# Gated linear attention followed by a tanh-shrink MLP: handing the tree products of a unit to the scheduler about a unit ahead

## The chip, the cores and the metric

One core of a Trainium2 chip. The metric is device time in microseconds (us), lower is better; every time below is of one run of the whole kernel or of its profiled execution. The engines are named as in the profile: PE (TensorE, matmuls and transposes), DVE (VectorE), ACT (ScalarE), POOL (GpSimd) and SP, whose queue issues all the DMAs of this kernel. TensorE's clock is granted at one of two levels, 1.2 or 2.4 GHz; the profile gives it as a share of 2.4 GHz.

## The reference

```python
# attention: B, H, S, D = 4, 8, 768, 48
for t in range(S):
    state = alpha[:, :, t, :, None] * state + np.einsum('bhd,bhe->bhde', k[:, :, t], v[:, :, t])
    y[:, :, t] = np.einsum('bhd,bhde->bhe', q[:, :, t], state)
# bridge
x = y.transpose(0, 2, 1, 3).reshape(B * S, H * D)          # 3072 x 384
# MLP: w_in 384 x 2048, w_out 2048 x 384, both float64 in memory
h = x @ w_in
g = h - np.tanh(h)
out = (g @ w_out).astype(np.float32)
```

## The kernel before, in words

The work is cut into 12 **units** of 256 tokens, three to a batch entry, numbered 0 to 11; a unit is two **chunks** of 128 tokens. For each unit there is a recurrence (`gla`) and an MLP (`moe`). The MLP of unit u needs the recurrence of unit u, and the recurrence of a unit needs the state left by the unit before it in the same batch entry.

The recurrence of a unit is a Python generator that yields after each step, 18 steps in all:

- **Tree** (lines 237 to 252, 8 steps). PE transposes `alpha` of both chunks (`tp<-ident,an`), ACT copies the result to `pre`, and POOL works through seven levels, at each multiplying halves of `suf` (L250) and of `pre` (L251): the cumulative products of alpha from the left and from the right. 14 POOL instructions of 128x512 in a chain, a copy among them, and a memset (L247, L248).
- **Ends** (lines 253 to 261, 1 step). DVE clamps the last products into `ends` (L254) and inverts them into `recs` (L257); POOL scales `suf` by `recs` (L259, two instructions).
- **Chunks** (lines 264 to 317, 4 steps each). PE transposes q and k of the chunk, DVE multiplies them with `pre` and `suf` into `qh` and `kh` (L267, L268), PE forms the scores `sc` (L274), DVE masks them into `x` (L278), PE transposes `kh` (L284), forms `y` from the old state (L291) and from `x` (L296) and the update `up` (L305), and the state is updated: DVE adds (L313), POOL multiplies by the chunk's end (L314, two halves). The first chunk of a batch entry has no old state (L316 on DVE alone), the last one needs no update.
- The last step also sends the transposed result to `xT` with DMAs (L324).

The MLP of a unit (`dense`) has 8 steps and a closing one. A step `s` computes `h` with PE (L119), then the activation on ACT and DVE; DVE's part per step is `w` (L127), `d` (L129), `z` (L132), `g` (L133) and `g` again (L134). Two steps later, `second(s)` multiplies `g` with `w_out` (L141) into `o`. There are two PSUM buffers for `h`, so `h` of a step can be written when `d` of the step two before it has been read.

Ahead of the MLP the float64 weights are decoded to float32 in 28 pieces (`load_w`): five DVE instructions (L181 to L188), two on ACT, one on POOL (`man`, L191), and a last one on DVE (L192).

Two things set the order. The code at line 335 gives each step a place in a list: the unit of place is one MLP step, an MLP with its closing step takes `MOE` = 9 places, unit u's MLP begins at place 9u, and all steps are emitted in the order of their places. Then a scheduler places what was emitted on each engine's queue, and may move an instruction ahead of earlier emitted ones where it reckons that it is ready; each engine then works through its queue strictly in that order. Before the change the 18 steps of a recurrence stand half a place apart:

```python
at = (u - 1) * MOE - EARLY
order += [(at + i * MOE / GLA, 0, "gla", u) for i in range(GLA)]
order += [(at - 4, 0, "load", u)]
```

Of the kernel before, what the change touches and what calls it, by code (L numbers as in the profile page):

```python
# [18 lines left out]
CU = 2  # L19
# [17 lines left out]
def kernel(  # L37
# [18 lines left out]
    LEVELS = 7  # L56
# [3 lines left out]
    FS = FT // 2  # L60
# [96 lines left out]
    def main(ctx):  # L157
# [174 lines left out]

        MOE, GLA, EARLY = FS + 1, 3 + LEVELS + 4 * CU, 5.0
        order = []
        for u in range(NU):
            order += [(u * MOE + i, 1, "moe", u) for i in range(MOE)]
            at = (u - 1) * MOE - EARLY
            order += [(at + i * MOE / GLA, 0, "gla", u) for i in range(GLA)]  # L340
            order += [(at - 4, 0, "load", u)]
        order += [(-MOE - EARLY + 2 + i, 2, "weights", 0) for i in range(2 * d_ff // 512)]
        make = {"moe": moe, "gla": gla, "load": load, "weights": lambda _: weights()}
# [130 lines left out]
    with ExitStack() as inner:  # L474
        main(inner)
# [52 lines left out]
```

## Time and profile before

| | before |
|---|---|
| time, median of 3 runs (lowest to highest) | 851.12 us (850.72 to 852.2) |
| time of the profiled execution | 853.7 us |
| its span, first to last instruction | 852.0 us |
| PE busy | 690.9 us (81%) |
| DVE busy | 555.4 us (65%) |
| ACT busy | 362.4 us (43%) |
| POOL busy | 295.4 us (35%) |
| mean granted TensorE clock | 0.914 |

The span is what the profile covers, and 1.7 us of the execution's time lie around it. Busy shares are averages over two stages that differ: to about 165 us the weights are decoded and PE is often idle; after that PE is busy nearly all the time but for a pause in each unit.

### The profile page before, as it was taken

What the parts mean: (1) busy time and instruction counts of PE and PEld (TensorE: products, weight loads), DVE (VectorE), ACT (ScalarE), POOL (GpSimd) and SP (SyncE); (2) the same over time, 40 slices, a digit from 0 to 9 for tenths busy, and PEclk for the clock granted to TensorE, in tenths of its full rate; (3) what the DMA queues carried; (4) which work ended last, traced back from release to release, by engine and by line L of the source; (5) the groups of instructions that cost most, each with busy time, mean ns of one, the idle gap of its engine ahead of it and who ended that gap; (6) DMA issues with size and microseconds to landing.
All of it is one profiled execution on the core that took longest, in us unless ns stands there. A gap on an engine that the chain in (4) does not pass through costs nothing.

```text
span 852.0 us, 10194 instructions
## 1 busy us (share of the span) xinstructions
PE 690.9 (81%) x3698; PEld 494.3 (58%) x3698; DVE 555.4 (65%) x818; ACT 362.4 (43%) x629; POOL 295.4 (35%) x281
## 2 busy tenths in 40 slices
PE   1172642697999979979989899799799799799995
PEld 1151431474767747747657567567577477577673
DVE  4979989966666557557467457556656656565573
ACT  2131331462645525615425435526444445355552
POOL 6739468272000630720710801802703604500000
PEclk9985765898999989989989989989899899899998
DMA  9571744500102202212112112013021000000000
GB/s 158 118 177 56 177 127 105 121 0 17 31 0 56 47 15 54 45 34 49 30 38 45 31 37 62 13 41 72 0 47 29 0 20 19 0 20 19 19 1 22
DMA packets 113911, 41.62 MB, mean 49 GB/s; under 512 B 102592, under 2 KB 110272, under 8 KB 113856
## 3 DMA queue, kind: packets, MB, share of 16 engines
q1 hardware_dynamic: 113856, 40.91, 21.2%
q8 instruction: 31, 0.51, 0.2%
q14 instruction: 24, 0.20, 0.1%
HBM read 31.46 MB, written 4.72 MB: 42 GB/s over the span
## 4 chain that ended last, share of the span: by engine, by line
PE 55%; POOL 20%; DVE 16%; ACT 3%; issue 3%; DMA 1%; SPq 1%; DVEq 0%; POOLq 0%; ACTq 0%
PE o L141 21%; PE h L119 20%; POOL pre L251 9%; POOL suf L250 9%; PE tp L234 4%; PE sc L274 3%; PE y L296 3%; PE y L291 2%; DVE g L134 2%; DVE e L186 2%; DVE e L184 2%; DVE g L133 2%; DVE e L181 1%; DVE w_in L192 1%; DVE m L188 1%
## 5 line engine op out<-in xcount | busy, mean ns | idle before, releaser
L141 PE MATMUL o<-w_out,g 128*128 128x384 f32 x768 | 284.2, 520 | 43.6 <-DVE g L134 42.9
L119 PE MATMUL h<-xT,w_in 128*128 128x256 f32 x1152 | 283.5, 390 | 22.8 <-DMA xT<-yT 14.2
L119 PEld LDWEIGHTS h<-xT,w_in 128*128 128x128 f32 x1152 | 215.5, 194 | 66.0 <-issue 13.6
L141 PEld LDWEIGHTS o<-w_out,g 128*128 128x128 f32 x768 | 154.5, 204 | 145.1 <-DVE g L134 49.5
L125 ACT ACTIVATE sq<-h 128x512 f32<-128x512 f32 x96 | 57.3, 597 | 192.7 <-PE h L119 153.4
L314 POOL TENSOR_TENSOR state<-state,pre 64x192 f32<-64x192 f32 x32 | 19.9, 622 | 314.4 <-DVE state L313 312.4
L127 DVE TENSOR_TENSOR w<-h,sq 128x512 f32<-128x512 f32 x96 | 65.8, 685 | 84.8 <-ACT th L126 84.8
L251 POOL TENSOR_TENSOR pre<-pre 128x512 f32<-128x512 f32 x84 | 97.9, 1166 | 5.3
L250 POOL TENSOR_TENSOR suf<-suf,pre 128x512 f32<-128x512 f32 x72 | 94.9, 1318 | 5.5
L134 DVE COPY_PREDICATED g<-large,d 128x512 f32<-128x512 int32 x96 | 86.7, 903 | 2.6
L132 DVE SCALAR_TENSOR_TENSOR z<-sq,z 128x512 f32<-128x512 f32 x96 | 71.1, 740 | 23.7 <-ACT z L130 23.7
L133 DVE SCALAR_TENSOR_TENSOR g<-z,w 128x512 f32<-128x512 f32 x96 | 81.7, 851 | 3.1
L131 ACT ACTIVATE large<-sq,m_bias 128x512 f32<-128x512 f32 x96 | 69.1, 720 | 5.6 <-DVE g L134 5.6
L128 ACT ACTIVATE z<-sq,z_bias 128x512 f32<-128x512 f32 x96 | 69.4, 723 | 2.9 <-DVE g L133 2.9
L130 ACT ACTIVATE z<-z,g_bias 128x512 f32<-128x512 f32 x96 | 68.7, 716 | 0.0
L234 PE MATMUL tp<-ident,kn 128*128 128x128 f32 x96 | 17.8, 315 | 59.9 <-DVE qh L267 59.9
L129 DVE TENSOR_TENSOR d<-h,th 128x512 f32<-128x512 f32 x96 | 65.2, 679 | 0.0
L126 ACT ACTIVATE th<-h 128x512 f32<-128x512 f32 x96 | 56.9, 593 | 0.0
L234 PEld LDWEIGHTS tp<-ident,kn 128*128 128x128 f32 x96 | 11.9, 156 | 67.7 <-DVE qh L267 61.2
L191 POOL TENSOR_TENSOR man<-man,low 128x384 f32<-128x384 f32 (+1 forms) x28 | 33.6, 1200 | 48.1 <-ACT man L189 48.1
L254 DVE TENSOR_SCALAR ends<-pre 128x8 f32<-128x8 f32 x12 | 2.0, 168 | 73.3 <-POOL pre L251 73.3
L189 ACT ACTIVATE man<-m 128x384 f32<-128x384 int32 (+1 forms) x28 | 15.9, 570 | 79.5 <-DVE m L188 79.5
(59 smaller groups left out, 603.0 us busy)
## 6 DMA issues: line engine op xcount, KB each, us to landing
raw<-in_moe_w_in_dram SPq DMA_DIRECT2D x12, 512.0 KB, 4.2
raw<-in_moe_w_out_dram SPq DMA_DIRECT2D x16, 384.0 KB, 3.2
an<-in_alpha_dram SPq DMA_DIRECT2D x24, 192.0 KB, 4.1
kn<-in_k_dram SPq DMA_DIRECT2D x24, 192.0 KB, 3.2
qn<-in_q_dram SPq DMA_DIRECT2D x24, 192.0 KB, 3.3
vn<-in_v_dram SPq DMA_DIRECT2D x24, 192.0 KB, 3.6
out_dram<-ob SPq DMA_DIRECT2D x24, 192.0 KB, 1.9
xT<-yT SPq DMA_DIRECT2D x72, 48.0 KB, 2.0
```

The costliest lines, as they stand in the source:

```text
L119: T.matmul(h[:, a, :], lhsT=w_in[:, j, f * P:(f + 1) * P], rhs=x_t[:, j, :], start=(j == 0), stop=(j == KT - 1))
L127: V.tensor_mul(w, h, sq)
L128: A.activation(z, sq, AF.Square, bias=z_bias, scale=ZA)
L129: V.tensor_sub(d, h, th)
L130: A.activation(z, z, AF.Square, bias=g_bias)
L131: A.activation(large, sq, AF.Relu, bias=m_bias)
L132: V.scalar_tensor_tensor(out=z, in0=sq, scalar=ZL, in1=z, op0=ALU.mult, op1=ALU.add)
L133: V.scalar_tensor_tensor(out=g, in0=z, scalar=ZC, in1=w, op0=ALU.add, op1=ALU.mult)
L134: V.copy_predicated(out=g, mask=large.bitcast(I32), data=d)
L141: T.matmul(o[c], lhsT=g[:, a * tu + c * P:a * tu + (c + 1) * P], rhs=w_out[:, f, :], start=(f == 0), stop=(f == FT - 1))
L250: GP.tensor_mul(s0, s0, e1)
L251: GP.tensor_mul(p1, p1, e0)
```

## The change

The 18 steps of a recurrence are split into two runs. The first 8 (the tree) are emitted from place 9(u-1) - 8 on, 0.4 places apart; the other 10 (ends, both chunks, the DMAs of xT) from place 9(u-1) on, also 0.4 apart. Before, all 18 were emitted from place 9(u-1) - 5 on, 0.5 apart. So the tree of unit u is now emitted among the chunk steps of unit u-1, whose places are 9(u-2) to 9(u-2) + 3.6. The loads of a unit stand 4 places ahead of its tree, as before, and so 3 places earlier than they did; the weights start 3 places earlier too. No instruction is added, removed or altered, and no buffer is added.

```diff
-        MOE, GLA, EARLY = FS + 1, 3 + LEVELS + 4 * CU, 5.0
+        MOE, TREE, CHUNK, EARLY = FS + 1, 1 + LEVELS, 2 + 4 * CU, 8.0
         order = []
         for u in range(NU):
             order += [(u * MOE + i, 1, "moe", u) for i in range(MOE)]
             at = (u - 1) * MOE - EARLY
-            order += [(at + i * MOE / GLA, 0, "gla", u) for i in range(GLA)]
+            order += [(at + 0.4 * i, 0, "gla", u) for i in range(TREE)]
+            order += [((u - 1) * MOE + 0.4 * i, 0, "gla", u) for i in range(CHUNK)]
             order += [(at - 4, 0, "load", u)]
```

What the scheduler makes of it is seen in the queues of the two built programs, at unit 8 as an example.

DVE's queue before, around the `ends` of unit 8, which stands between `d` and `z` of an MLP step:

```order
L127 TENSOR_TENSOR w<-h,sq 128x512
L129 TENSOR_TENSOR d<-h,th 128x512
L254 TENSOR_SCALAR ends<-pre 128x8
L257 RECIPROCAL recs<-ends 128x8
L132 SCALAR_TENSOR_TENSOR z<-sq,z 128x512
L133 SCALAR_TENSOR_TENSOR g<-z,w 128x512
L134 COPY_PREDICATED g<-large,d 128x512
```

DVE's queue now at the same instruction (`x_3358` and `x_3359` are the masked scores of the second chunk of unit 7):

```order
L132 SCALAR_TENSOR_TENSOR z<-sq,z 128x512
L278 TENSOR_TENSOR x_3358<-sc_3348,keep 128x512
L278 TENSOR_TENSOR x_3359<-sc_3349,keep 128x512
L133 SCALAR_TENSOR_TENSOR g<-z,w 128x512
L254 TENSOR_SCALAR ends<-pre 128x8
L134 COPY_PREDICATED g<-large,d 128x512
L257 RECIPROCAL recs<-ends 128x8
L127 TENSOR_TENSOR w<-h,sq 128x512
L129 TENSOR_TENSOR d<-h,th 128x512
```

The `ends` of unit 8 was emitted at place 63, after the chunks of unit 7; the scheduler has moved it forward, into the second chunk of unit 7, ahead of the last instruction of an MLP step.

POOL's queue before, from the state products of unit 7 (`state_91` of its first chunk, `state_90` of its second) to the start of the tree of unit 8:

```order
L259 TENSOR_TENSOR suf<-suf,recs 128x512 x2
L314 TENSOR_TENSOR state_91<-state_91,pre 64x4x48 x2
L314 TENSOR_TENSOR state_90<-state_90,pre 64x4x48 x2
L247 COPY suf<-pre 128x512
L248 MEMSET suf 128x512
L251 TENSOR_TENSOR pre<-pre 128x512
L250 TENSOR_TENSOR suf<-suf,pre 128x256x2
```

POOL's queue now, from the start of the tree of unit 8:

```order
L247 COPY suf<-pre 128x512
L251 TENSOR_TENSOR pre<-pre 128x512
L250 TENSOR_TENSOR suf<-suf,pre 128x256x2
L314 TENSOR_TENSOR state_91<-state_91,pre 64x4x48
L251 TENSOR_TENSOR pre<-pre 128x256x2
L314 TENSOR_TENSOR state_91<-state_91,pre 64x4x48
L250 TENSOR_TENSOR suf<-suf,pre 128x128x4
```

The tree of unit 8 now begins ahead of the state products of unit 7's first chunk, which stand inside it; those of the second chunk stand behind the whole tree and the scaling of `suf`.

PE's queue before at the transposes of `an` (alpha) of unit 8, between MLP steps:

```order
L234 MATMUL tp<-ident,an_72 128x128 x4
L119 MATMUL h<-xT,w_in 128x256 x2
L234 MATMUL tp<-ident,an_72 128x128 x4
L119 MATMUL h<-xT,w_in 128x256 x4
```

PE's queue now at the same transposes (`x_3249` and `x_3250` are the masked scores of the first chunk of unit 7):

```order
L284 MATMUL tp<-ident,kh 128x128 x4
L291 MATMUL y<-qh,state_90 64x128 x8
L296 MATMUL y<-x_3249,vn_79 64x128
L234 MATMUL tp<-ident,an_72 128x128 x4
L296 MATMUL y<-x_3250,vn_79 64x128
...
L234 MATMUL tp<-ident,an_72 128x128 x4
L296 MATMUL y<-x_3250,vn_79 64x128
```

They have moved to where unit 7's first chunk forms its `y`. From the second of them to the `second` step that needs the `g` behind `ends`, PE's queue now holds three MLP `h` steps (L119), two `second` steps (L141), and of unit 7's recurrence two `up` (L305), the transposes of q and k, the scores, the transposes of `kh` and both parts of `y` of the second chunk.

In the first part of the program, the tree of unit 3 now stands among the last weights on POOL and DVE; before, only units 0 to 2 stood there and unit 3's came after the last weight. Unit 4 takes the place there that unit 3 had.

## Rows read from the trace of the kernel before

**Rows 1.** Waits of the whole span: us in total, times, longest us.

```profile
DVE ends L254 <- POOL pre L251: 73.3, 9, 9.2
PE o L141 <- DVE g L134: 42.9, 8, 5.5
```

**Rows 2.** Timeline of DVE from 395 to 432 us: start, us, idle before and releaser.

```profile
425.58 0.17 DVE L254 TENSOR_SCALAR ends<-pre 128x8 f32<-128x8 f32 x1 [8.01 <-POOL pre L251]
...
428.02 1.45 DVE L134 COPY_PREDICATED g<-large,d 128x512 f32<-128x512 int32 x1
...
431.99 0.73 DVE L134 COPY_PREDICATED g<-large,d 128x512 f32<-128x512 int32 x1
```

**Rows 3.** Timeline of POOL from 395 to 432 us: one unit's tree.

```profile
407.60 0.65 POOL L247 COPY suf<-pre 128x512 f32<-128x512 f32 x1 [16.27 <-ACT pre L239]
...
412.51 1.60 POOL L250 TENSOR_TENSOR suf<-suf,pre 128x512 f32<-128x512 f32 x1
...
424.49 1.06 POOL L251 TENSOR_TENSOR pre<-pre 128x512 f32<-128x512 f32 x1
```

**Rows 4.** Timeline of PE from 366 to 432 us, around the same tree.

```profile
406.19 0.66 PE L234 MATMUL tp<-ident,an 128*128 128x128 f32 x4
...
421.33 2.75 PE L119 MATMUL h<-xT,w_in 128*128 128x256 f32 x12
429.52 2.92 PE L141 MATMUL o<-w_out,g 128*128 128x384 f32 x4 [5.44 <-DVE g L134]
```

**Rows 5.** Chain that ended last: start, us, what; `x8` and `x12` are one MLP step.

```profile
307.01 10.72 PE o L141 x24
...
369.01 10.44 PE o L141 x24
...
776.06 2.58 PE o L141 x8
778.64 2.59 PE h L119 x12
```

**Rows 6.** Stretches of 1 us: engines' busy time, granted clock, DMA share, GB/s.

```profile
428.00:429.00 1.00, 0.00 (x0) 0.00 (x0) 0.98 (x1) 0.72 (x1) 0.88 (x1) 0.78 0.00 0
...
729.00:730.00 1.00, 0.67 (x3) 0.05 (x1) 0.00 (x0) 1.00 (x2) 0.92 (x2) 1.00 0.00 0
732.00:733.00 1.00, 0.00 (x0) 0.00 (x0) 0.00 (x0) 0.00 (x0) 0.92 (x2) 0.68 0.00 0
```

**Rows 7.** Chain that ended last, 380 to 400 us: pieces of a chunk.

```profile
383.34 0.59 PE tp L284 x4
...
388.62 0.60 PE up L305 x16
...
390.28 0.44 PE tp L234 x4
...
391.58 0.57 PE tp L234 x4
...
393.88 1.09 PE sc L274 x16
...
397.75 1.02 PE y L291 x16
398.78 0.87 PE y L296 x16
```

**Rows 8.** Groups of instructions of the whole span, by line: busy, mean ns.

```profile
L314 POOL TENSOR_TENSOR state<-state,pre 64x192 f32<-64x192 f32 x32 | 19.9, 622 | 314.4 <-DVE state L313 312.4 <-PE tp L234 1.3
L267 DVE TENSOR_TENSOR qh<-tp,pre 128x512 f32<-128x512 f32 x24 | 16.5, 688 | 36.8 <-PE tp L234 36.1
L259 POOL TENSOR_TENSOR suf<-suf,recs 128x512 f32<-128x512 f32 x24 | 33.4, 1408 | 7.6 <-DVE recs L257 7.6
```

**Rows 9.** Stretches of 20 us while weights are decoded: PE, PEld, DVE, ACT, POOL busy.

```profile
40.00:60.00 20.00, 14.56 (x107) 11.02 (x108) 17.34 (x39) 7.70 (x14) 5.89 (x6) 0.91 0.78 178
60.00:80.00 20.00, 7.55 (x42) 4.95 (x41) 17.81 (x17) 3.51 (x7) 19.30 (x18) 0.59 0.27 78
```

## The prediction

> **What bounds the kernel now.** I read the page first, then the chain that ended last, then the waits, then the timelines of DVE, POOL and PE side by side over one unit. The kernel has two stages. Once the weights are decoded, PE is the bound: the chain runs through its matmuls, one MLP step of `h` in 2.59 us and one of `o` in 2.58 [rows 5], with one hole per unit. Ahead of that DVE is the bound: in the 20 us from 60 it is busy for 17.81 and PE for 7.55 [rows 9].
>
> The hole is made by one instruction. DVE waits 73.3 us in all, in nine waits, at `ends` (L254) for POOL's tree [rows 1]. In the unit shown POOL starts the tree at 407.60 and ends it at 425.55, 18.0 us; DVE has nothing before it but 8.01 us of waiting, though the MLP's own `z`, `g`, `g` stand right behind it. They end at 429.47, 3.9 us after `ends` began [rows 2, 3]. PE ran without a gap to 424.08 and then waits 5.44 us for that `g` [rows 4]. The clock goes too: it falls to 1.2 GHz within the pause, so that the 24 `o` matmuls behind it take 10.44 to 10.72 us, where 3 x 2.58 = 7.74 is the full-clock price [rows 5]. One hole therefore costs 5.44 + 2.85 = 8.3 us; nine of them (units 3 to 11), 74.7 us.
>
> **The change, part by part.** No instruction is added, so the terms are moved waits.
>
> *The nine old holes* go: -74.7 us.
>
> *New holes.* "A unit ahead" holds for the tree in the list, but the queues show that the scheduler pulls `ends` forward too: the tree starts in the first chunk of the unit before, `ends` stands in the second. So DVE still waits, and the question is what PE has to do meanwhile. I count from A, the start of the second half of the `an` transposes, for unit 8.
>
> - Tree ready: before, POOL began 407.60 - 406.19 = 1.4 us after A and took 18.0 [rows 3, 4]. Now two state products of 0.62 us and two gaps stand inside it [rows 8]: A + 1.4 + 18.0 + 1.4 = A + 20.8. Behind `ends` (0.17) there is now just one `g` (0.73 where POOL is not in its way) [rows 2] before PE has what it needs: A + 21.8. Before it was A + 23.3.
> - PE's work from A to that point: three `h` steps 7.8, two `second` 5.2 [rows 5], two `up` 1.2, the transposes of q, k and `kh` 1.6, scores 1.1, both parts of `y` 1.9, and the `an` transposes with a row of `y` 0.6 [rows 7]: 19.4, so PE is free at A + 19.4. Before it was 424.08 - 406.19 = 17.9 [rows 4].
> - Hole: 21.8 - 19.4, about 2.4 us instead of 5.44.
>
> Units 5, 8 and 11 are like that: 3 x 2.4 = 7.2. For units 6 and 9 the unit before is the last of its batch entry and has no second `up` and no `kh` transposes (1.2 us less cover): 2 x 3.6 = 7.2. For units 7 and 10 `ends` stands behind the whole MLP step and there is no state product in the tree, so PE has one more `second` to do; I bound this hole by 0 and one `second` (2.58) and take 1.3: 2.6. Unit 4 sits where unit 3 sat, after the last weight, with nothing new to cover it: the old 8.3.
>
> What is queued behind the waiting `ends`: `g`, `recs`, and the `w` and `d` that free the next `h` buffer. `w` and `d` come within 2 us, inside PE's 2.58 us of `second`. On POOL, the first chunk's state products wait for DVE's add; `y` of the second chunk needs them. Behind a copy, three products of the tree and their own 2 x 0.62 us they are done at about A + 7.5, and PE's work ahead of that `y` fills it to A + 9. The products of the second chunk now stand behind the whole tree and the scaling (2.8 us); they are needed a unit later, some 30 us on. SP's loads keep their distance to the tree, and xT's DMAs come at the same place as before: nothing.
>
> *The clock in the new holes.* It fell in the two pauses shown at some 4.5 us in (pause from 424.08, mean 0.78 in 428 to 429) and at 2.7 us in (pause from 729.67, mean 0.68 in 732 to 733) [rows 4, 6]. A 2.4 us hole is below both, a 3.6 us one lies between. I count one fall of the two: +2.9. Bounds: none (0), all five (14).
>
> *The weights stage.* One more tree (unit 3's) and half a unit of chunks now stand in it. While a tree runs, DVE gets through 17 instructions in 20 us; without one, 39 [rows 9]: it loses 22 x 17.34/39 = 9.8 us of work in 20, so about 9 per tree. The added half unit is four DVE instructions of 0.69 us and one scaling of 2.8 [rows 8], +5; against that, chunk work now stands under trees where DVE and POOL used to take turns, which I value at -4. I take +10. Bounds: 0, if that overlap pays for the tree, and 23, if DVE loses the whole 18 and the 5.
>
> The Trainium skill (SBUF — State Buffer, Who interferes with whom) speaks against the change here: VectorE and GpSimd share a port pair as an exclusive lock, whoever starts first holds it for the whole instruction, and the other fully blocks. By that rule a tree among decode work costs DVE its full length, the term is the upper bound, 23, and the time that of rival B. The trace agrees only in part, since DVE still does 17 instructions where the rule at its strictest leaves none.
>
> *Half a unit less later.* A period of 62.0 us (369.01 - 307.01) less 8.3 less the MLP's 8 x 5.17 leaves 12.3 us of recurrence on PE; the next, 60.5 us, leaves 10.8 [rows 4, 5]. Half of it is done in the weights stage where PE is idle: -5.8.
>
> **Sum.** -74.7 + (7.2 + 7.2 + 2.6 + 8.3) + 2.9 + 10 - 5.8 = -42.3. Against the profiled execution: 853.7 - 42.3 = 811.4 (span 809.7). The median of the runs is 2.6 below the profiled one, so 851.1 - 42.3 = **809 us**, 5.0% faster.
>
> **Rivals.**
>
> - *A: PE does not see the wait at all in units 5 to 11.* For it: the tree has stretches at 1.06 and at 1.60 us per product [rows 3], and while DVE stands still POOL has no rival; 3 us off the tree would close the holes. Against it: the 18.0 us hold 8 us of such standing already. Time: 809 - 17.0 - 2.9 = 789.
> - *B: the weights stage pays in full*, +23. For it: POOL is busy 19.30 of 20 us there and DVE, the bound, does under half as much [rows 9]. Against it: in the new queue 16 of the 28 weight pieces still have their POOL part between trees. Time: 822; with a clock fall in all five larger holes, 833.
> - *C: the change does not do what it says*: `ends` follows the tree and each of eight holes costs the old 8.3. For it: DVE's wait in the new place should be as long as before, near 9 us. Against it: the count of cover above. Time: 851.1 - 8.3 + 10 - 5.8 = 847.
> - *D, slower.* The tree is stretched by what now runs beside it. If the ten products behind the state products went at 1.6 us instead of 1.1, the tree would be ready 5 us later, every hole would be 5 us longer and long enough for the clock to fall: 3 x 10.3 + 2 x 11.5 + 2 x 9.2 + 8.3 = 80.6, time 851.1 - 74.7 + 80.6 + 10 - 5.8 = 861. It decides from a mean of (74.7 - 8.3 - 4.2)/7 = 8.9 us per hole in units 5 to 11. Against it: DVE stands still in that very stretch, as before.
>
> **Chances.** Forecast 0.58, A 0.17, B 0.14, C 0.05, D 0.06. The range reaches from A to B: 788 to 831, and leaves out C and D and a little of B. A measurement of this kernel tells 0.2% from no change. Faster by more: 0.92 (forecast, A, B, C, less a little), within it 0.02, slower 0.06 (D).
>
> **What would show it.** In the profile after: DVE's wait at `ends` still 50 to 70 us in all, but PE's waits for `g` down from 42.9 to 15 to 25 us; in the steady stage a granted clock of 1.0 through most units; one larger hole at unit 4; PE's dense stretch beginning about 10 us later than before, at 175 to 180 us; periods of 56 us instead of 61. Wrong would be: PE idle over 5 us per unit (C or D), no idle at all (A), or a weights stage that ends at 190 us (B).

## The result, and the profile after

The changed kernel takes 819.59 us (median of 4 runs, 817.96 to 820.56), the kernel before beside it 851.66 us (850.72 to 852.78): ratio 0.9621, 95% interval 0.96 to 0.9642, so 3.8% faster. The forecast was 809 us with a range of 788 to 831: the time lies inside it, 10.6 us above the number. The profiled execution took 820.56 us, its span 818.9 us (before 852.0).

**The waits.** The whole span first, then the waits of PE between 210 and 730 us (us in total, times, longest), where before had 38.1 us in 7 waits for `g`.

```profile
DVE ends L254 <- POOL pre L251: 74.6, 10, 9.6
```

```profile
PE o L141 <- DVE g L134: 5.4, 6, 1.8
PE y L296 <- DVE x L278: 4.7, 6, 1.9
PE tp L234 <- ACT ks L285: 1.5, 6, 0.3
```

DVE waits as long for POOL's tree as in [rows 1]: 74.6 us for 73.3. What fell is PE's wait behind it. The change did not shorten the wait; it put it where PE has other work. Two new, small waits of PE stand in its place: for the masked scores `x` and for `ks`.

**One unit.** POOL's, DVE's and PE's timelines around the tree of unit 9 (start, us, idle before and releaser); [rows 2, 3, 4] show such a tree before.

```profile
555.93 0.66 POOL L247 COPY suf<-pre 128x512 f32<-128x512 f32 x1 [31.60 <-ACT pre L239]
...
559.24 0.51 POOL L314 TENSOR_TENSOR state<-state,pre 64x192 f32<-64x192 f32 x1
...
573.52 1.06 POOL L251 TENSOR_TENSOR pre<-pre 128x512 f32<-128x512 f32 x1
```

```profile
574.61 0.17 DVE L254 TENSOR_SCALAR ends<-pre 128x8 f32<-128x8 f32 x1 [9.58 <-POOL pre L251]
574.69 0.73 DVE L134 COPY_PREDICATED g<-large,d 128x512 f32<-128x512 int32 x1
```

```profile
553.71 0.88 PE L296 MATMUL y<-x,vn 128*64 128x128 f32 x12
554.52 0.66 PE L234 MATMUL tp<-ident,an 128*128 128x128 f32 x4
555.10 0.43 PE L296 MATMUL y<-x,vn 128*64 128x128 f32 x2
...
570.92 2.75 PE L119 MATMUL h<-xT,w_in 128*128 128x256 f32 x12
575.47 2.85 PE L141 MATMUL o<-w_out,g 128*128 128x384 f32 x8 [1.80 <-DVE g L134]
```

Count as the forecast did, from the second half of the `an` transposes, A = 554.52. POOL starts 1.4 us after A, two state products stand inside the tree (the first at 559.24), and it ends at 574.58 (573.52 + 1.06), A + 20.1; `ends` waits 9.58 us, the one `g` behind it takes 0.73, and PE resumes at A + 20.95 (forecast A + 21.8). PE has work to 573.67 (575.47 - 1.80), A + 19.15; the forecast for this unit was A + 18.2, the 19.4 of unit 8 less 1.2. The hole is 1.80 us, where 3.6 was forecast and 5.44 stood before. Note too what PE does at A: the `an` transposes stand inside the `y` of the first chunk and cut it into pieces.

**The clock.** The same timeline and DVE's in unit 7 (windows of before have their like in [rows 6]), then the granted clock (the last column but two) behind it.

```profile
448.91 1.09 PE L291 MATMUL y<-qh,state 128*64 128x128 f32 x14
451.85 0.43 PE L296 MATMUL y<-x,vn 128*64 128x128 f32 x2 [1.85 <-DVE x L278]
452.45 1.09 PE L296 MATMUL y<-x,vn 128*64 128x128 f32 x14 [0.16 <-DVE x L278]
453.46 4.53 PE L119 MATMUL h<-xT,w_in 128*128 128x256 f32 x12
```

```profile
446.91 1.05 DVE L132 SCALAR_TENSOR_TENSOR z<-sq,z 128x512 f32<-128x512 f32 x1
447.99 1.65 DVE L133 SCALAR_TENSOR_TENSOR g<-z,w 128x512 f32<-128x512 f32 x1
449.67 1.55 DVE L134 COPY_PREDICATED g<-large,d 128x512 f32<-128x512 int32 x1
451.12 1.27 DVE L278 TENSOR_TENSOR x<-sc,keep 128x512 f32<-128x512 f32 x2
```

```profile
453.00:454.00 1.00, 1.00 (x9) 0.79 (x6) 0.00 (x0) 0.43 (x1) 0.92 (x2) 0.74 0.00 0
454.00:456.00 2.00, 2.00 (x6) 1.59 (x5) 0.00 (x0) 0.16 (x1) 2.00 (x3) 0.50 0.10 27
...
520.00:577.00 57.00, 54.80 (x305) 39.49 (x304) 34.58 (x57) 29.06 (x51) 23.26 (x23) 1.00 0.21 45
```

In units 7 and 10 the masked scores `x` stand behind `z`, `g`, `g`, and these take 1.05, 1.65 and 1.55 us because the tree of the next unit runs beside them on POOL (0.69 to 0.75 a little earlier, alone). PE waits 1.85 us for `x`, the clock falls to 1.2 GHz and one `h` step takes 4.53 us instead of 2.75. From 520 to 577 us, a stretch that begins just behind unit 8's small hole (0.59 us) and holds unit 9's 1.80 us, it stays at 2.4 GHz.

**The start of the dense stretch**, and unit 4's hole, on PE:

```profile
178.60 5.42 PE L119 MATMUL h<-xT,w_in 128*128 128x256 f32 x12 [0.81 <-DVE d L129]
...
207.62 4.51 PE L119 MATMUL h<-xT,w_in 128*128 128x256 f32 x12 [5.07 <-DVE d L129]
```

The stretch begins at 178.60 us; before it was 167.85. Unit 4 has the hole that unit 3 had.

**Where the time went, in two pieces.** From its first `h` to the end of the program, each kernel's dense stretch as one row (us long, then PE busy; DVE's is the third): before, after.

```profile
167.85:852.00 684.15, 625.69 (x3222) 447.13 (x3222) 412.00 (x604) 317.45 (x550) 192.62 (x176) 0.95 0.13 28
```

```profile
178.60:818.90 640.30, 611.88 (x3174) 440.09 (x3174) 384.67 (x598) 313.78 (x547) 173.16 (x159) 0.98 0.13 30
```

PE's idle time falls from 58.46 (684.15 - 625.69) to 28.42 us, -30.0; its busy time falls by 13.8; the stretch starts 10.75 later. Together -33.1, the difference of the spans.

### The profile page after: what moved, and what is told of

Its sections match the earlier page's. It is cut to its first block, busy times and chain, and to the rows that moved or that the text cites. A ratio compares the mean times of both kernels' runs of the same rounds, so it can differ in the third digit from the quotient of the medians.

```text
span 818.9 us, 10180 instructions
## 1 busy us (share of the span) xinstructions
PE 687.1 (84%) x3698; PEld 494.8 (60%) x3698; DVE 538.6 (66%) x818; ACT 360.1 (44%) x629; POOL 297.8 (36%) x281
## 4 chain that ended last, share of the span: by engine, by line
PE 47%; POOL 21%; DVE 17%; ACT 7%; issue 5%; DMA 1%; SPq 1%; DVEq 0%; POOLq 0%; ACTq 0%
PE h L119 24%; PE o L141 18%; POOL pre L251 8%; POOL suf L250 8%; POOL man L191 2%; PE tp L234 2%; DVE g L134 2%; ACT z L130 2%; DVE g L133 2%; DVE z L132 2%; ACT th L126 2%; DVE m L188 2%; PE y L296 2%; ACT z L128 1%; DVE e L183 1%
## 5 line engine op out<-in xcount | busy, mean ns | idle before, releaser
L119 PE MATMUL h<-xT,w_in 128*128 128x256 f32 x1152 | 279.6, 391 | 6.3 <-DVE d L129 5.9
L141 PE MATMUL o<-w_out,g 128*128 128x384 f32 x768 | 265.4, 489 | 6.5 <-DVE g L134 5.4
L119 PEld LDWEIGHTS h<-xT,w_in 128*128 128x128 f32 x1152 | 220.0, 195 | 53.0 <-issue 11.0
L141 PEld LDWEIGHTS o<-w_out,g 128*128 128x128 f32 x768 | 143.1, 190 | 97.7 <-DVE g L134 15.0
L247 POOL COPY suf<-pre 128x512 f32<-128x512 f32 x12 | 8.4, 701 | 257.0 <-ACT pre L239 257.0
L132 DVE SCALAR_TENSOR_TENSOR z<-sq,z 128x512 f32<-128x512 f32 x96 | 67.2, 700 | 25.7 <-ACT z L130 25.7
L133 DVE SCALAR_TENSOR_TENSOR g<-z,w 128x512 f32<-128x512 f32 x96 | 74.5, 776 | 2.8
L134 DVE COPY_PREDICATED g<-large,d 128x512 f32<-128x512 int32 x96 | 74.2, 773 | 2.7
L234 PE MATMUL tp<-ident,kn 128*128 128x128 f32 x96 | 18.1, 316 | 52.7 <-DVE qh L267 52.7
L189 ACT ACTIVATE man<-m 128x384 f32<-128x384 int32 (+1 forms) x28 | 15.9, 569 | 99.5 <-DVE m L188 99.5
L296 PE MATMUL y<-x,vn 128*64 128x128 f32 x384 | 37.9, 295 | 18.1 <-DVE x L278 15.3
L254 DVE TENSOR_SCALAR ends<-pre 128x8 f32<-128x8 f32 x12 | 3.9, 324 | 74.6 <-POOL pre L251 74.6
L267 DVE TENSOR_TENSOR qh<-tp,pre 128x512 f32<-128x512 f32 x24 | 16.5, 689 | 48.8 <-PE tp L234 48.5
```

The source lines that it names most:

```text
L119: T.matmul(h[:, a, :], lhsT=w_in[:, j, f * P:(f + 1) * P], rhs=x_t[:, j, :], start=(j == 0), stop=(j == KT - 1))
L132: V.scalar_tensor_tensor(out=z, in0=sq, scalar=ZL, in1=z, op0=ALU.mult, op1=ALU.add)
L133: V.scalar_tensor_tensor(out=g, in0=z, scalar=ZC, in1=w, op0=ALU.add, op1=ALU.mult)
L134: V.copy_predicated(out=g, mask=large.bitcast(I32), data=d)
L141: T.matmul(o[c], lhsT=g[:, a * tu + c * P:a * tu + (c + 1) * P], rhs=w_out[:, f, :], start=(f == 0), stop=(f == FT - 1))
```

## The experiments

Each was timed beside the kernel before; the ratio is to that, with its 95% interval, and the changed kernel's 819.59 us is 0.9621 on that scale. The first four ran together (before: 853.41 us), the last four together (before: 853.5 us).

**1. `ends` on POOL, in the kernel before.** If DVE does not wait for the tree, no instruction of the MLP can stand behind that wait. POOL clamps and inverts instead (a power of -1, from a constant tile):

```diff
-            V.tensor_scalar(out=ends[:, u, :].unsqueeze(2), in0=whole, scalar1=END_MIN,
+            GP.tensor_scalar(out=ends[:, u, :].unsqueeze(2), in0=whole, scalar1=END_MIN,
...
-            V.reciprocal(recs, ends[:, u, :])
+            GP.tensor_tensor(out=recs, in0=ends[:, u, :], in1=minus, op=ALU.pow)
```

> The kernel before, with the clamp and the reciprocal of the tree's ends moved from VectorE to GpSimd (the reciprocal as a power of -1), so that no VectorE instruction waits for the tree itself; the order of steps is that of before. Theory (a hole in TensorE's work comes from VectorE standing at that instruction with the MLP's g behind it): all nine holes close. From the rows of after, a hole was worth 5.44 us of idling plus some 2.4 us of slow clock, less 0.3 us that TensorE then waits at the end of a unit anyway, 7.5 us each, so about 851.7 - 67 = 784 us, below the changed kernel. Rival (the wait only moves: the scaled suffix products come too late and VectorE stands at kh in place of ends): 830 us or more, with VectorE idle at kh for about as long as it was at ends.

Measured: 804.19 us (800.06 to 808.01), 0.9443 (0.9413 to 0.9473). The wait of DVE is what made the holes: without it, and with every instruction in its old place, the kernel is faster than the changed one. The rival is out: no wait of DVE at `kh` for POOL is left in the trace. But 784 was missed by 20 us. The timelines of DVE, POOL and PE at the end of a unit's MLP show the larger part of why (line numbers are two higher here):

```profile
405.80 0.68 DVE L131 TENSOR_TENSOR d<-h,th 128x512 f32<-128x512 f32 x1
406.40 1.52 DVE L134 SCALAR_TENSOR_TENSOR z<-sq,z 128x512 f32<-128x512 f32 x1
407.95 1.43 DVE L135 SCALAR_TENSOR_TENSOR g<-z,w 128x512 f32<-128x512 f32 x1
409.42 1.47 DVE L136 COPY_PREDICATED g<-large,d 128x512 f32<-128x512 int32 x1
```

```profile
407.45 1.39 POOL L252 TENSOR_TENSOR suf<-suf,pre 128x512 f32<-128x512 f32 x1
408.91 1.39 POOL L253 TENSOR_TENSOR pre<-pre 128x512 f32<-128x512 f32 x1
...
411.05 1.67 POOL L259 TENSOR_TENSOR recs<-ends,minus 128x8 f32<-128x8 f32 x1
```

```profile
410.94 2.85 PE L143 MATMUL o<-w_out,g 128*128 128x384 f32 x8 [1.20 <-DVE g L136]
414.91 2.85 PE L143 MATMUL o<-w_out,g 128*128 128x384 f32 x8 [1.13 <-DVE g L136]
```

The tree now runs beside a DVE that works. `z`, `g`, `g` take 1.43 to 1.52 us each (`d`, which reads PSUM, still 0.68), POOL's products 1.39 instead of the 1.06 of [rows 3], and PE waits 1.20 and 1.13 us for `g` at the end of a unit, where it has no chunk work left. Between 210 and 730 us it waits so 15 times, 12.0 us, where the expectation had allowed 0.3 us a unit.

**2. The same in the changed kernel.**

> The changed kernel with the same move of the ends to GpSimd. Theory: what the changed kernel still loses at ends goes: the pause at unit 4 (5.07 us and about 1.9 of slow clock) and the five small ones (0.56, 1.80, 0.59, 1.80, 0.20), 12 us in all, so about 808 us; and it is then slower than the kernel before with the same move, since the longer weights stage (10.7 us) and the finer mixing on TensorE stay. Rival (TensorE's remaining time is not bound by that wait at all): within 3 us of 820.

Measured: 812.33 us (811.75 to 812.77), 0.9526 (0.9507 to 0.9544). So the waits for `ends` that are left in the changed kernel are worth some 7 us, net of a dense stretch that starts at 184.24 instead of 178.60. That later start, which the expected 808 did not have, is more than the 4 us by which it was missed; that the kernel is slower than experiment 1 came true. PE's wait for `x` in units 7 and 10 is not touched:

```profile
446.41 0.43 PE L298 MATMUL y<-x,vn 128*64 128x128 f32 x2 [1.82 <-DVE x L280]
...
448.81 3.71 PE L121 MATMUL h<-xT,w_in 128*128 128x256 f32 x12
```

1.82 us, and the `h` behind it at 3.71: this wait comes from the tree beside DVE's products, not from `ends`.

**3. The new places from unit 4 on only**; units 0 to 3 and the weights where they were:

```diff
-            order += [(at + 0.4 * i, 0, "gla", u) for i in range(TREE)]
-            order += [((u - 1) * MOE + 0.4 * i, 0, "gla", u) for i in range(CHUNK)]
+            if u > 3:
+                order += [(at + 0.4 * i, 0, "gla", u) for i in range(TREE)]
+                order += [((u - 1) * MOE + 0.4 * i, 0, "gla", u) for i in range(CHUNK)]
+            else:
+                at += 3
+                order += [(at + 0.5 * i, 0, "gla", u) for i in range(TREE + CHUNK)]
             order += [(at - 4, 0, "load", u)]
-        order += [(-MOE - EARLY + 2 + i, 2, "weights", 0) for i in range(2 * d_ff // 512)]
+        order += [(-MOE - 5.0 + 2 + i, 2, "weights", 0) for i in range(2 * d_ff // 512)]
```

> Units 0 to 3 and the weights in the places of before, units 4 to 11 in the new places. Theory: TensorE's dense stretch starts again at about 168 us instead of 178.6 (-10.7), half a unit of recurrence goes back behind the weights (+4.5), unit 3 has the old hole (+7.5), unit 4's hole falls from some 7 to some 2 us (-5): about 816 us. Rival (the later start is due to something other than the tree among the weights, or the tree there is free): 826 us or more.

Measured: 813.46 us (812.44 to 814.43), 0.9533 (0.9513 to 0.9553): 2.5 us under the expectation, 6 us under the changed kernel, and the rival is out. The dense stretch starts where it did before, and unit 4's hole shrinks; unit 3 has its old one again:

```profile
168.07 4.25 PE L119 MATMUL h<-xT,w_in 128*128 128x256 f32 x12 [3.40 <-DVE d L129]
...
198.17 5.48 PE L141 MATMUL o<-w_out,g 128*128 128x384 f32 x8 [4.87 <-DVE g L134]
```

```profile
286.89 2.85 PE L141 MATMUL o<-w_out,g 128*128 128x384 f32 x8 [1.33 <-DVE g L134]
```

**4. The new places up to unit 4 only** (the same edit with `u < 5`, the weights in their new place).

> Units 0 to 4 and the weights in the new places, units 5 to 11 in those of before: the weights stage of the changed kernel with the steady stage of before. Theory: 851.7 + 10.7 - 4.5 = about 858 us, slower than before, so that the whole gain of the change is in the steady stage. Rival (the start is where part of the gain comes from): 847 us or less.

Measured: 852.91 us (851.5 to 854.37), 0.9997 (0.9983 to 1.0012): -0.5 us, no difference, where some 6 us more had been expected. The expectation had left out that eight holes stand here (unit 4's and those of units 5 to 11) where before had nine. With that: +10.75 for the start, -4.0 for chunk work done ahead of the stretch, -7.8 for one hole less (both worked out below): about -1. PE behind the tree of unit 5:

```profile
368.98 1.65 PE L141 MATMUL o<-w_out,g 128*128 128x384 f32 x2 [5.84 <-DVE g L134]
```

So what the change pays and gains in the first units cancels, and its whole gain lies in units 5 to 11. By experiment 3 units 0 to 3 are better left where they were (0.9533 against the changed kernel's 0.9621).

**5. Half of the change: the tree early**, ends and chunks at their old places:

```diff
             order += [(at + 0.4 * i, 0, "gla", u) for i in range(TREE)]
-            order += [((u - 1) * MOE + 0.4 * i, 0, "gla", u) for i in range(CHUNK)]
+            order += [(at + 7 + 0.5 * i, 0, "gla", u) for i in range(CHUNK)]
```

> One part of the change alone: the tree from place 9(u-1) - 8 on, 0.4 apart, as in the changed kernel; ends and chunks at 9(u-1) - 1, 0.5 apart, where they were before. In the queues ends again stands in the second chunk of the unit before, but ahead of two g products instead of one. Theory (the gain comes from where the waiting ends stands: PE then has chunk work that needs no g): the gain stays but for one more g product (0.7 us) per hole in seven units, 819.6 + 5 = 825 us, 816 to 831. Rival (the gain comes from taking the chunks away from the end of the MLP): 845 us or more, with PE waiting 5 us or more for g in each unit.

Measured: 804.85 us (804.61 to 805.53), 0.9436 (0.9416 to 0.9457). The rival is out, and my number was 20 us too high: this half alone gains more than the whole change. DVE and PE in unit 7, then PE's dense stretch as one row (compare the two rows of before and after above):

```profile
450.79 0.17 DVE L254 TENSOR_SCALAR ends<-pre 128x8 f32<-128x8 f32 x1 [8.05 <-POOL pre L251]
```

```profile
427.03 1.09 PE L296 MATMUL y<-x,vn 128*64 128x128 f32 x16
428.06 0.66 PE L234 MATMUL tp<-ident,an 128*128 128x128 f32 x4
...
438.29 2.10 PE L141 MATMUL o<-w_out,g 128*128 128x384 f32 x6
...
452.38 2.85 PE L141 MATMUL o<-w_out,g 128*128 128x384 f32 x8 [1.33 <-DVE g L134]
```

```profile
181.17:803.00 621.83, 600.40 (x3146) 432.02 (x3146) 392.98 (x596) 311.88 (x544) 167.12 (x153) 0.99 0.13 30
```

`ends` still waits 8.05 us, and PE sees 1.33 of it. Against the changed kernel the stretch starts 2.6 us later, PE is idle for 7.0 us less (21.43) and busy for 11.5 less: -15.9, the difference of the spans (803.0 and 818.9). Three costs of the changed kernel are gone here. PE has 2.10 us of `o` at 438.29 between the scores of the second chunk and their `y`, where the changed kernel had nothing of the MLP, so it does not wait for `x` in units 7 and 10 and no `h` step is slow there. The chunk is one place further on when the `an` transposes come, so `y` stands in one piece ahead of them (427.03, x16). And unit 4 has no hole: POOL starts its tree at 171.71 us, still among the weights (187.51 in the changed kernel), and `ends` comes at 193.56 without a wait, where the changed kernel lost 5.07 us and 1.8 of slow clock. Against this stand the holes of units 5 to 11, 10.2 us here and 5.4 there. The rows of `y` from `x` in the dense stretch, of before, of the changed kernel and of this one (PE busy, instructions; the engine alone):

```profile
167.85:852.00 684.15, 20.36 (x288) 0.95 0.13 28
```

```profile
178.60:819.00 640.40, 24.47 (x272) 0.98 0.13 30
```

```profile
181.17:803.00 621.83, 20.00 (x272) 0.99 0.13 30
```

That is 71 ns a matmul, 90 ns and 74 ns.

**6. The other half: the chunks later**, the tree at its old place (`at += 3`, the tree 0.5 apart, the chunks as in the changed kernel, the weights where they were before).

> The other part alone: tree from place 9(u-1) - 5 on, 0.5 apart, as before; ends and chunks from 9(u-1) on, 0.4 apart, as in the changed kernel. In the queues ends stands near the end of the MLP again, between d and z. Theory: the nine holes of some 5.4 us and the slow clock behind them stay, the dense stretch starts near 168 us, and the time is that of the kernel before within 1 per cent, 845 to 858 us. Rival (chunks away from the end of the MLP are enough): 830 us or less.

Measured: 856.96 us (855.74 to 857.42), 1.0039 (1.0025 to 1.0054), 0.4% slower. `ends` stands at the end of the MLP as in [rows 2], and the hole is all there, on DVE and on PE:

```profile
427.30 0.17 DVE L254 TENSOR_SCALAR ends<-pre 128x8 f32<-128x8 f32 x1 [8.01 <-POOL pre L251]
```

```profile
431.24 10.14 PE L141 MATMUL o<-w_out,g 128*128 128x384 f32 x24 [5.44 <-DVE g L134]
```

The row of `y` from `x`, as in experiment 5:

```profile
166.54:855.50 688.96, 24.81 (x304) 0.95 0.13 29
```

82 ns a matmul, with transposes of q inside `y` here: the dearer `y` comes with the chunks' move, also where the tree is not early.

So the two halves do not add: one alone is worth -48.7 us, the other +3.5, both together -32.

**7. Experiment 3 with `ends` on POOL.**

> Two edits together: units 0 to 3 and the weights in the places of the kernel before, units 4 to 11 in those of the changed kernel, and ends and recs computed by POOL, so that DVE does not wait for the tree. Theory (costs add): from the 813.5 us of the late-from-unit-4 run take unit 3's whole hole (7.5), unit 4's 1.3 and some 5 of small holes: 800 us, 796 to 804; the waits for x in units 7 and 10 stay. Rival (POOL's tree, no longer alone while DVE stands still, slows DVE at the unit's end as in the run of before with ends on POOL): 804 us or more.

Measured: 802.02 us (798.53 to 804.04), 0.9409 (0.9386 to 0.9432): inside what the sum of costs gives, and not to be told from experiment 1. `o` waits for `g` nowhere after 190 us, so the rival's mechanism is not there; the waits for `x` stay, as in experiment 3.

**8. Experiment 1 with the whole recurrence two places earlier from unit 4 on** (`if u > 3: at -= 2`).

> The kernel before with ends and recs on POOL, and from unit 4 on the whole recurrence two places earlier (from place 9(u-1) - 7 on, 0.5 apart). Theory: what is left in the run with ends on POOL alone (804.2 us) is PE's two waits of some 1 us for g at a unit's end, which come from the tree running beside z and g there; two places earlier PE has chunk work at that point, and 8 units gain 1 to 1.5 us each: 792 to 797 us. Rival (the tree costs DVE the same wherever it runs, and PE sees it all the same): 803 us or more.

Measured: 795.2 us (793.88 to 796.09), 0.9321 (0.9298 to 0.9345), the fastest of all, 24 us under the changed kernel. Waits of PE between 210 and 730 us, and DVE beside the tree:

```profile
PE tp L236 <- DVE qh L269: 7.0, 8, 1.1
PE sc L276 <- DVE kh L270: 4.2, 8, 0.6
```

```profile
400.02 1.53 DVE L134 SCALAR_TENSOR_TENSOR z<-sq,z 128x512 f32<-128x512 f32 x1
...
403.05 1.50 DVE L136 COPY_PREDICATED g<-large,d 128x512 f32<-128x512 int32 x1
```

No wait for `g` is left in this window, though `z`, `g`, `g` are as slow as in experiment 1: the tree costs DVE the same, but PE has chunk work at that point. PE now waits 11.2 us for `qh` and `kh` instead, nearly as much as the 12.0 before, so the shorter waits for `g` are not the gain. By the profiled spans that is 5.3 us (798.3 to 793.0), by the medians 9. In the dense stretch PE is idle 0.7 us less and starts 0.7 later, but is busy 5.3 us less (605.51 to 600.20) with the same 3218 matmuls. So the time came out as expected, but not by the sum expected; why PE is busy for less stays open.

## Why the prediction was right, and where it was off

**Right: the mechanism.** `ends` still waits; PE has chunk work behind the wait. In unit 9 the count of cover from A held to within 1 us on either side: the tree is ready earlier than forecast, and PE is free later. Experiments 5 and 6 show it from both sides: where `ends` moves into the second chunk, the holes shrink to 0.9 to 2.1 us; where it stays at the end of the MLP they stay at 5.4 to 5.8. Rival C (the dear wait stays) and D (slower) are out by this; A (no wait seen) by the holes of 0.56, 1.80, 0.59, 1.80 and 0.20 us in units 5, 6, 8, 9 and 11; B (the weights stage pays in full) by the start at 178.60.

**Right: the weights stage**, +10 forecast, +10.75 measured. That it came so near is in part luck: of its terms, +9, +5 (4 x 0.69 + 2.8 adds up to 5.6) and -4, the last had no row behind it, and no run takes them apart. The bound of 23, a tree that stops DVE for its whole length, was not reached. The forecast took it for what the Trainium skill's rule gives (SBUF — State Buffer, Who interferes with whom), and read that rule too strictly: by the section the first to issue holds the shared ports for one instruction, not for a chain, and a DVE instruction with at most one SBUF input, outside the two-port modes, does not contend with GpSimd. The trace of experiment 1 agrees with both: DVE's and POOL's products end in turn there, and `d`, which has one operand in PSUM, keeps its 0.68 us.

**Off: the size.** Forecast -42.3, the spans say -33.1. In the pieces of the dense stretch:

| | forecast | measured |
|---|---|---|
| start of the stretch | +10 | +10.75 |
| PE idle: 9 x 5.44 less new holes | -26.5 | -30.0 |
| PE busy: clock (-25.7 + 2.9 + 2.9) and half a unit (-5.8) | -25.7 | -13.8 |
| sum | -42.2 | -33.1 |

The term that failed is **"Half a unit less later", -5.8**. The work did move: in the dense stretch 12 transposes of `an`, q and k are gone (208 to 196), 16 score matmuls, 4 transposes of `kh` and 16 of `y`. But the recurrence that is left became dearer. To see by how much, take each PE matmul of the two traces from its start to the start of the next one, or to its own end where a pause follows; then nothing is counted twice, and the sum is PE's busy time. The lines of the recurrence (L234, L274, L284, L291, L296, L305) go from 94.0 to 99.4 us, +5.4. At before's means the work that moved is worth 4.0, so the rest costs 9.5 more. That is 11.2 of the 11.9 us by which PE's busy time fell short. `o` fell by 18.8 us and `h` by 0.4, near the forecast's 19.9 for the clock.

Nearly all of the 9.5 lies in `y` from `x` (+5.1), in the transposes (+2.4) and in `y` from the old state, which stands ahead of the new wait for `x` (+1.1). Transposes stand inside `y` now, and the traces show what the change from one kind of matmul to the other costs. Where no pause follows, a `y` from `x` has the next `y` 63 ns behind it, but a transpose only after 203; a transpose has the next one after 119 ns, but a `y` or an `up` only after 202. Before's dense stretch has none of these changes; the changed kernel has 14 of the one kind and 22 of the other, some 4 us. The forecast showed this mixing in PE's queue and gave it no price. Experiments 5 (74 ns a matmul, no transposes inside `y`) and 6 (82 ns, transposes inside `y`, no early tree) bear it out.

**Off, and nearly even: the holes.** An old hole cost 5.44 and 2.35 of slow clock (18.8 us of `o` over the eight that are gone), 7.8, not 8.3. The new holes of units 5, 6, 8, 9 and 11 were smaller too: 5.0 us together, where 3 x 2.4 + 2 x 3.6 = 14.4 had been forecast, so that in this rival A's "none" was the nearer number. In units 7 and 10 the hole of 1.3 at `g` did not come; a wait of 2.2 us for `x` (0.35 and 1.85) and 1.8 us of slow clock came in its place, which the forecast did not have: it counted `w` and `d` behind the waiting `ends`, not the `x` behind the slowed `z` and `g`.

**What would show it.** DVE's wait of 50 to 70: 74.6, not shorter at all. PE's wait for `g` of 15 to 25: 5.4, or 10.5 with unit 4's hole, which the profile books under `d`. The clock at 1.0 through most units, the larger hole at unit 4, the start at 175 to 180, and the periods of 56 (55.9; 58.6 at units 7 and 10): seen.

## What to carry to other kernels

An engine that waits in order costs what stands behind it, so look first at where the waiting instruction stands in its queue and what the bounding engine can do meanwhile: here the wait stayed at 74 us and the time fell by 32. When a change moves two groups of steps, try each alone: the tree's move gave all of the gain, and moving the chunks with it took 15 us back, through mixed matmuls, through a wait for scores with no MLP work to cover it and through unit 4's hole behind the weights. Giving the waiting instruction to the engine that it waits for was worth as much here as covering the wait (804.2 and 804.9 us), and with the recurrence two places earlier as well the kernel was the fastest of all (795.2).

## What the hardware showed that was not expected

- Beside POOL's tree, DVE's products of two SBUF operands take up to 1.65 us instead of 0.69, and POOL's last ones 1.39 instead of 1.06; DVE's `w` and `d`, with one operand in PSUM, stay at 0.68 (experiment 1). The rows look like turns: DVE's products end at 407.92, 409.38 and 410.89, POOL's at 408.84 and 410.30. Both engines lose, and neither stands still for a whole chain.
- Pauses of PE of nearly one length end differently: after 1.80 us (575.47) the clock stays at 2.4 GHz, after 1.85 and then 0.16 us (451.85) it falls, and in experiment 5 a step behind a pause of 2.06 us (396.22) took 4.54 us, at a granted clock of 0.50 from 397 to 399. The forecast had counted a hole of 2.4 us as one without a fall.
- POOL inverts 128x8 values by a power of -1 in 1.67 us, where DVE's reciprocal takes 0.2; in experiment 1 one wait of 0.3 us is all that the profile puts down to it.
